# Fillers on an idle TensorE: from full products to short groups of transposes

## The chip, the core and the metric

The kernel runs on one core of a Trainium2 chip. The metric is the device time of one execution in microseconds (us). Before the change it is 1080.59 us, the median of 2 runs (1079.84 and 1081.34).

## The reference

A recurrent attention (RWKV-7) over 4 batches, 8 heads, 768 steps and a head size of 40 is followed by a gated feed-forward layer with 320 inputs and 1536 hidden units, all of it in fp32:

```python
for t in range(S):
    kt, vt, rt = (k[:, :, t], v[:, :, t], r[:, :, t])
    wt, at, bt = (w[:, :, t], a[:, :, t], b[:, :, t])
    y[:, :, t] = np.einsum('bhd,bhde->bhe', rt, state)
    Sa = np.einsum('bhde,bhe->bhd', state, at)
    state_decay = state * wt[:, :, None, :] - np.einsum('bhd,bhe->bhde', Sa, bt)
    state = state_decay + np.einsum('bhd,bhe->bhde', vt, kt)
...
rms = np.sqrt(np.mean(x * x, axis=-1, keepdims=True) + 1e-06)
xn = x / rms * rms_g
g = xn @ w_gate
silu = g * (1.0 / (1.0 + np.exp(-g)))
return (silu * (xn @ w_val) @ w_out)
```

Each batch and head has a state of 40 x 40 numbers; x is y with the heads of a time step side by side, 3072 rows of 320. The feed-forward weights come as 64-bit numbers, which the kernel narrows to fp32 itself.

## The kernel before

The 768 steps are cut into 24 chunks of 32. For each chunk there are four stages. `front` loads the chunk, turns it by transposes, and builds by levels (1, 2, 4, 8, 16 steps) the products between steps of the chunk: at each level TensorE multiplies `Ab` with `K` (a product on 40 rows and 64 columns), VectorE and ScalarE take the result into `LT` and `KN`, and make the `K` and `Ab` of the next level from those of this one. `inverse`, in the first chunks `early_inverse`, inverts a small triangular matrix of each sequence on VectorE. `main` takes the state through the chunk, forms y, normalizes it and transposes it into `xg`. After every second chunk `feed` multiplies 256 rows with the gate, value and output weights; that is most of TensorE's work. `narrow` makes the fp32 weights while the first chunks run.

Nothing is issued while these functions run. Each call of `tt`, `copy`, `pe` and so on adds a piece to a `Plan`. `Plan.issue` then walks through the text `ORDER`, which was written out ahead: each word is the place of the next piece among those left. It fixes the order on each engine, and there is no scheduler behind it. A word `-` stands for a filler: `self.warm()` is called, and one product goes to TensorE between two useful pieces. There are 151 such words in 33 runs of 1 to 14, all in the first quarter of the text. `PAIRS` says which of three pairs of PSUM banks each piece uses.

The filler is line 1017: the product of the identity with itself, 128 rows by 128 columns, accumulated into columns 320 to 447 of the first bank of `po`. `feed` uses columns 0 to 319 of both banks of `po` for its output; nothing ever reads the filler's columns. They are set to zero once, on line 519. An engine works through its queue in order, so a useful product behind fillers starts when they have gone through and its inputs are there.

Useful products are issued by line 488 (`mm`) and transposes by line 491 (`flip`); in fp32 a product is two instructions on TensorE and a transpose is one. Each has its own load of weights (LDWEIGHTS). Lines 446, 466, 469 and 472 are the helpers of VectorE and ScalarE.

Of the kernel before, what the change touches and what calls it, by code (L numbers as in the profile page):

```python
# [17 lines left out]
P = 128  # L18
# [352 lines left out]
def kernel(  # L371
# [33 lines left out]
    nc = tc.nc  # L405
    B, H, S, D = r.shape
    assert B == 4 and H == 8 and S % (CG * C) == 0 and D == 40
    DM = H * D
# [25 lines left out]
    def side(t, l, x):  # L434
# [4 lines left out]
    plan = Plan([psum.tile([P, 2, 512], FP32, name=f"ps{i}") for i in range(3)],  # L439
                [dram.tile([P, 2, 512], FP32, name=f"room{i}") for i in range(8)])  # L440
# [59 lines left out]
    ident = const.tile([P, P], FP32, name="ident")  # L500
# [15 lines left out]
    po_ = psum.tile([P, 2, 512], FP32, name="po")  # L516
    for t in plan.pairs[:2]:
        nc.vector.memset(t, 0.0)
    nc.vector.memset(po_[:, 0, DM:DM + P], 0.0)
    nc.scalar.copy(plan.pairs[2], plan.pairs[0])  # L520

    gcol = const.tile([P, KT], FP32, name="gcol")
# [107 lines left out]
    TOP = 64 + D  # L630
# [383 lines left out]
            front(c + 2)  # L1014
            (early_inverse if c + 2 < EARLY else inverse)(c + 2)

    plan.warm = lambda: nc.tensor.matmul(po_[:, 0, DM:DM + P], ident, ident, start=False, stop=False, skip_group_check=True)
    with tc.manual_schedule():
        plan.issue(ORDER, PAIRS)

# [29 lines left out]
```

## Time and profile before

| | before |
|---|---|
| median of the runs | 1080.59 us |
| the profiled execution: span from its first to its last instruction | 1078.2 us |
| TensorE busy (products) | 1010.2 us, 94% |
| TensorE busy (weight loads) | 828.3 us, 77% |
| VectorE, ScalarE, GpSimd busy | 834.2, 462.2, 309.0 us |
| mean granted clock of TensorE | 0.980 |
| fillers: product instructions | 302, first at 3.3 us, last at 233.9 us |
| duration of one such instruction (least, median, most) | 273, 275, 582 ns |
| fillers, busy | 47.3 us |

The profile holds one execution. Busy time counts each instruction with its latency, so instructions that follow each other closely overlap: the time from start to start is shorter than the duration. A row of the timeline merges instructions of one kind that follow each other, with the start of the first, the time to the end of the last, and their number; a bracket tells how long the engine stood idle before and what ended it. PEclk is the share of TensorE's full clock that was granted; the view in stretches gives its mean over each stretch. Ahead of the clock's first record, at 8.32 us, that view shows 1.00, though the instructions there have the durations of half the clock.

### The profile page before, as it was taken

What the parts mean: (1) busy time and instruction counts of PE and PEld (TensorE: products, weight loads), DVE (VectorE), ACT (ScalarE), POOL (GpSimd) and SP (SyncE); (2) the same over time, 40 slices, a digit from 0 to 9 for tenths busy, and PEclk for the clock granted to TensorE, in tenths of its full rate; (3) what the DMA queues carried; (4) which work ended last, traced back from release to release, by engine and by line L of the source; (5) the groups of instructions that cost most, each with busy time, mean ns of one, the idle gap of its engine ahead of it and who ended that gap; (6) DMA issues with size and microseconds to landing.
All of it is one profiled execution on the core that took longest, in us unless ns stands there. A gap on an engine that the chain in (4) does not pass through costs nothing. (4 is left out here: it accounts for less than half of the span.)

```text
span 1078.2 us, 53465 instructions
## 1 busy us (share of the span) xinstructions
PE 1010.2 (94%) x23406; PEld 828.3 (77%) x23406; DVE 834.2 (77%) x2861; ACT 462.2 (43%) x1043; POOL 309.0 (29%) x554
## 2 busy tenths in 40 slices
PE   6767899999999999999999999998999999999998
PEld 6766778777888787877788778887777887887776
DVE  7887879876868888887897888887788889797420
ACT  6845756643543433532443434433344344342211
POOL 9714404120532223241331331331332331200000
PEclk9778999999999999999999999999999999999999
DMA  9965448766564364574465654665545553744242
GB/s 180 196 155 123 73 106 220 213 127 177 124 142 122 99 150 116 144 145 120 96 152 133 146 126 112 142 142 123 126 106 110 134 150 90 162 109 123 77 140 86
DMA packets 172456, 143.34 MB, mean 133 GB/s; under 512 B 125504, under 2 KB 143872, under 8 KB 172224
## 3 DMA queue, kind: packets, MB, share of 16 engines
q1 hardware_dynamic: 153856, 116.96, 42.4%
q0 software_dynamic: 16192, 22.64, 12.2%
q8 instruction: 184, 3.01, 1.2%
q10 hardware_dynamic: 2176, 0.33, 0.2%
q14 instruction: 48, 0.39, 0.1%
HBM read 123.86 MB, written 15.99 MB: 130 GB/s over the span
## 5 line engine op out<-in xcount | busy, mean ns | idle before, releaser
L488 PE MATMUL ps<-xg,wf 128*128 128x256 f32 (+1 forms) x1728 | 355.2, 392 | 4.7 <-DVE xg L446 1.1
L488 PEld LDWEIGHTS ps<-xg,wf 128*128 128x128 f32 (+1 forms) x1728 | 261.6, 189 | 60.4 <-issue 16.9
L488 PE MATMUL po<-wf,hT 128*128 128x320 f32 x576 | 180.1, 445 | 0.1
L446 DVE TENSOR_TENSOR tmp<-Yi,M 128x60 f32<-128x60 f32 (+24 forms) x620 | 129.5, 209 | 19.7 <-DMA M<-sB 6.9
L446 DVE TENSOR_TENSOR Yi<-Yi,tmp 128x60 f32<-128x60 f32 (+24 forms) x620 | 130.2, 210 | 12.7 <-DVE ss L446 0.2
L466 ACT ACTIVATE sg<-ps 128x256 f32<-128x256 f32 x144 | 52.4, 383 | 192.4 <-PE ps L488 182.7
L488 PEld LDWEIGHTS po<-wf,hT 128*128 128x128 f32 x576 | 102.6, 191 | 34.0 <-issue 1.7
L485 POOL DMA_DIRECT2D VU<-in_v_dram x92 | 53.6, 587 | 234.2 <-PE ps L488 157.0
L446 DVE TENSOR_TENSOR hT<-ps,sg 128x256 f32<-128x256 f32 x144 | 59.0, 419 | 62.4 <-ACT sg L466 55.9
L469 ACT COPY KN<-ps 128x640 f32<-128x640 f32 x96 | 66.2, 691 | 76.6 <-PE ps L491 27.9
L488 PEld LDWEIGHTS ps<-Ab,K 40*64 40x64 f32 x4608 | 78.3, 139 | 26.4 <-issue 8.5
L446 DVE TENSOR_TENSOR K<-K,T 128x512 f32<-128x512 f32 (+1 forms) x192 | 93.3, 495 | 4.2 <-ACT K L469 2.1
L488 PE MATMUL ps<-Ab,K 40*64 40x56 f32 x4608 | 88.0, 225 | 8.8 <-ACT K L469 3.7
L485 POOL DMA_DIRECT2D kbn<-in_b_dram x92 | 53.4, 584 | 147.9 <-PE ps L488 147.0
L446 DVE TENSOR_TENSOR As<-ps,msi 128x256 f32<-128x256 f32 (+1 forms) x186 | 79.2, 475 | 18.3 <-PE ps L488 17.4
L469 ACT COPY K<-K 128x256 f32<-128x256 f32 (+1 forms) x168 | 71.8, 443 | 41.3 <-PE ps L488 20.3
L488 PEld LDWEIGHTS ps<-As,KN 128*40 128x40 f32 x3072 | 64.6, 122 | 15.1 <-issue 9.7
L485 POOL DMA_DIRECT2D wn<-in_w_dram x92 | 51.6, 565 | 83.7 <-DVE KN L446 34.7
L485 POOL DMA_DIRECT2D kbn<-in_k_dram x92 | 53.5, 585 | 73.8 <-PE ps L488 73.5
L488 PE MATMUL ps<-As,KN 128*40 128x32 f32 x3072 | 71.1, 203 | 3.7 <-issue 2.7
L446 DVE TENSOR_TENSOR y<-y,ps 128x256 f32<-128x256 f32 x119 | 49.9, 419 | 19.7 <-PE ps L488 17.6
L446 DVE COPY_PREDICATED LT<-near,ps 128x384 f32<-128x384 uint32 (+2 forms) x72 | 52.3, 727 | 3.6 <-PE ps L488 1.9
(133 smaller groups left out, 1544.5 us busy)
## 6 DMA issues: line engine op xcount, KB each, us to landing
wf<-sW SPq DMA_DIRECT2D x144, 480.0 KB, 4.3
M<-sB SPq DMA_DIRECT2D x80, 128.0 KB, 3.8
rn<-in_r_dram SPq DMA_DIRECT2D x24, 160.0 KB, 4.5
sW<-ex SPq DMA_DIRECT2D x16, 240.0 KB, 4.3
out_dram<-o SPq DMA_DIRECT2D x48, 80.0 KB, 3.9
kbn<-in_k_dram POOLq DMA_DIRECT2D x92, 40.0 KB, 3.5
kbn<-in_b_dram POOLq DMA_DIRECT2D x92, 40.0 KB, 3.3
wan<-in_a_dram POOLq DMA_DIRECT2D x46, 80.0 KB, 4.7
```

What stands on the lines that cost most here:

```text
L446: plan.add("DVE", kind, lambda at: fn(at(o), *m(at)), [o], aps(*args))
L466: plan.add("ACT", "act", lambda at: nc.scalar.activation(at(o), at(a), f, **kw), [o] + aps(acc), [a])
L469: plan.add("ACT", "copy", lambda at: nc.scalar.copy(at(o), at(a)), [o], [a])
L485: plan.add(by, "dma", lambda at: queue.dma_start(out=o, in_=i), [o], [i])
L488: return o, lhsT, rhs, lambda at: nc.tensor.matmul(at(o), lhsT, rhs, start=start, stop=stop, skip_group_check=True)
```

## The change

Each filler becomes a group of transposes of the identity, marked as transposes (`is_transpose`). Five kinds take turns, four fillers of each kind before the next. `D` is 40, `TOP` 104 and `P` 128.

| kind | rows | result rows | instructions of one filler |
|---|---|---|---|
| 1 | 64 | 128 | four of 64 columns, on the lower and upper 64 rows by turns |
| 2 | 40 | 128 | four of 40 columns, by turns as well |
| 3 | 64 | 104 | four of 64 columns, by turns as well |
| 4 | 64 | 104 | four of 64 columns, all on the lower 64 rows |
| 5 | 128 | 104 | one of 128 columns |

Those on the upper rows write to the second bank of `po`, so the memset of line 519 covers both banks. The words `-` stay where they are, and all other pieces and their order are unchanged on each engine.

```diff
-    nc.vector.memset(po_[:, 0, DM:DM + P], 0.0)
+    nc.vector.memset(po_[:, :, DM:DM + P], 0.0)
...
-    plan.warm = lambda: nc.tensor.matmul(po_[:, 0, DM:DM + P], ident, ident, start=False, stop=False, skip_group_check=True)
+    turns = [(64, P, 0), (D, P, 0), (64, TOP, 0), (64, TOP, 1), (P, TOP, 0)]
+
+    def warm():
+        kind = plan.fillers // 4 % len(turns)
+        plan.fillers += 1
+        rows_, cols, alone = turns[kind]
+        for _ in range(2 if rows_ < P else 1):
+            for i in range(1 if rows_ == P else 2):
+                u = 0 if alone else i
+                at = slice(u * 64, u * 64 + rows_)
+                nc.tensor.matmul(po_[0:cols, u, DM:DM + rows_], ident[at, 0:cols], ident[at, at], start=False, stop=False,
+                                 is_transpose=True, skip_group_check=True)
+
+    plan.fillers = 0
+    plan.warm = warm
```

## The prediction

> **What bounds the kernel now.** I read the page first (share of each engine, the span in 40 slices), then the groups of line 1017, which issues the fillers, then busy time in stretches of 3.41 us, then the timeline of TensorE around the runs of fillers. The page's chain of waits reaches back only to 785 us and consists mostly of TensorE's own products; it says nothing of the first 235 us, where all fillers lie, so that part is read from the stretches.
>
> From the page, a slice being 27 us:
>
> ```profile
> PE   6767899999999999999999999998999999999998
> DVE  7887879876868888887897888887788889797420
> PEclk9778999999999999999999999999999999999999
> ```
>
> TensorE is bound from the sixth slice on. In the first four it is not: it waits there for VectorE and ScalarE, and its granted clock is at 0.7 to 0.8. The same run in stretches of 3.41 us (busy time of each engine with its count, then the clock):
>
> ```profile
> core 0: us, PE busy (x) PEld busy (x) DVE busy (x) ACT busy (x) POOL busy (x), PEclk, DMA share, GB/s
> 25.39:28.80 3.41, 1.78 (x16) 1.79 (x17) 3.27 (x7) 3.34 (x8) 3.22 (x7) 1.00 1.20 242
> 32.22:35.63 3.41, 2.13 (x101) 1.64 (x101) 3.41 (x9) 3.41 (x10) 3.16 (x12) 1.00 1.04 240
> 35.63:39.04 3.41, 3.41 (x82) 3.08 (x78) 3.16 (x7) 3.35 (x8) 3.06 (x8) 0.50 0.69 154
> 49.28:52.70 3.42, 1.68 (x15) 1.49 (x14) 0.77 (x5) 3.36 (x8) 0.00 (x0) 1.00 1.10 278
> 73.18:76.59 3.41, 0.78 (x64) 0.69 (x64) 2.93 (x15) 0.26 (x1) 0.00 (x0) 1.00 0.60 136
> 76.59:80.00 3.41, 2.88 (x98) 2.46 (x99) 0.19 (x2) 0.80 (x3) 0.00 (x0) 0.50 0.89 280
> 83.42:86.83 3.41, 3.18 (x72) 2.67 (x72) 2.49 (x5) 3.32 (x5) 0.42 (x1) 0.50 0.16 15
> 86.83:90.24 3.41, 2.90 (x144) 2.56 (x145) 2.53 (x10) 3.38 (x7) 2.10 (x5) 1.00 0.53 131
> ```
>
> The clock changes only at these edges, between full and half. What decides is the streaming time, not busy time with its latency: a product instruction of n columns streams for 0.84 ns times n at full clock (128 columns: 107 ns, below), twice that at half. I counted it, overlaps once, for all stretches of the trace. Those after which the clock fell streamed 13, 31, 32, 32, 43 and 43% of the stretch; the lowest after which it stayed were 42, 44, 46, 47, 48%. At half clock it rose again after stretches with 82% or more and stayed down after 79% and less, and once after 86%. So the border is the same number of columns: 43% at full, some 85% at half clock. The stretches at 25.39, 49.28 and 69.76 stand at 47, 42 and 44%, of which fillers are 41, 42 and 44.
>
> What a product costs is read from the timeline (start, length of the merged row, tile, rows*columns of the weights, count):
>
> ```profile
> 28.57 1.04 PE L491 MATMUL ps<-ident,kbn 128*104 128x128 f32 x8
> 40.19 1.95 PE L491 MATMUL ps<-ident,wan 128*104 128x128 f32 x8
> 54.40 0.71 ACT L469 COPY K<-K 128x256 f32<-128x256 f32 x2 [0.24 <-DVE K L446]
> 53.91 2.27 PE L1017 MATMUL po<-ident 128*128 128x128 f32 x18
> 56.12 1.15 PE L488 MATMUL ps<-Ab,K 40*64 40x56 f32 x64
> 115.51 1.14 PE L488 MATMUL ps<-rE,vut 40*64 40x32 f32 x64 [0.21 <-ACT vut L469]
> 136.81 1.14 PE L488 MATMUL ps<-xg,wf 64*128 64x256 f32 x8
> 140.64 3.72 PE L488 MATMUL ps<-xg,wf 128*128 128x256 f32 x16
> ```
>
> A full transpose is one instruction: (1.04 - 0.27) / 7 = 0.11 us, at half clock (1.95 - 0.45) / 7 = 0.21. A filler is two instructions of 0.12 us: (2.27 - 0.28) / 17. Products on 64 rows run two side by side: (1.14 - 0.40) / 7 = 0.106 us against (3.72 - 0.39) / 15 = 0.222 on 128 rows.
>
> **The change part by part.** *Removed*: 151 fillers of two instructions at 0.115 us, some 34.7 us of TensorE. *Added*: 520 transposes for the same 151 places. The kind changes after every four fillers, so the five kinds come 32, 32, 31, 28 and 28 times. A transpose of 64 columns streams 0.055 us. Its weights of 128 columns must be loaded too: loads last 130 ns for 104 columns and 141 for 128, so 0.46 ns a column, 0.059 us for 128. That loads can be the limit is seen at 115.51: four side by side, (1.14 - 0.22) / 63 * 4 = 58 ns each, where 32 columns stream 27 ns. So a 64- or 40-row transpose takes about 0.06 us, and two halves side by side make a group of four 0.12 us. The fourth kind stays on one half, 0.24; the fifth is one full transpose, 0.11. Sum: 95 * 0.12 + 28 * 0.24 + 28 * 0.11 = 21.2 us. Transposes on 64 rows do not occur in this trace; were they not side by side, it would be 95 * 0.24 + 9.8 = 32.6. I take 21.2, since the nearest row, the 64-row products, overlaps. Either way they have no consumer; what counts is what follows.
>
> *TensorE is free earlier* (gain). At 56.12 the product starts when the fillers end, 1.0 us after its last input, the ScalarE copies that end at 55.11. Compared in this way with their last release, useful steps behind fillers start late by 1.0 (56.12), 0.9 (101.96), 0.75 (28.57), 0.7 (78.78), 0.6 (9.12), 0.6 (118.17) and 0.6 us (188.87), and all others together 1.2: 6.4 us. Some five of them go. Behind the remaining runs the input is late anyway, and shorter fillers only lengthen the wait.
>
> *The clock* (loss). Stretches whose fillers carry the border fall below it, and the next one runs at half clock, where useful streaming takes twice as long. At the start (3.3 us) fillers end at 5.1 instead of 6.85, TensorE waits for the load of wan, and the clock rises one stretch later: useful streaming there is 1.0 us, so +1.0. At 25.39 the fillers go from 41 to some 32%: next stretch +2.3. At 49.28 from 42 to 22%: +1.0. At 69.76 from 44 to 20-33%: +0.5. About even are 15.15 (60 to 43%, +2.2 at stake), 83.42 (82%, just at the upper border, so any shift of the starts decides; +2.1) and 192.64 (70 to 43%, +1.7); less likely 172.16 (61 to 45%, +1.7). With halves and a quarter: 4.8 + 3.0 + 0.4 = 8.2 us.
>
> *Code*. The page's instruction queue moved 184 packets for 46,812 TensorE instructions, one for some 256. In the first 250 us its weight loads wait for "issue" 37 times, 20.0 us, 0.54 each. 436 more instructions are 1.7 packets: +0.9 us at most, nothing if it falls into a wait; I take 0.5.
>
> *Memset*. One VectorE instruction of twice the columns ahead of the first filler; the first useful step waits for its load until 6.8 us in any case. Nothing. No wait, DMA or step on another engine is added or moved.
>
> *How much reaches the end.* In the front stage the next level's K is made by VectorE and ScalarE without TensorE; a product there only feeds LT and KN. With VectorE at 3.2 to 3.4 of 3.41 us in most of these stretches, some delay of TensorE is hidden, as is some gain. Between none and all I take half for both: -2.5 + 4.1 + 0.5 = +2 us. The profiled execution has a span of 1078.2, the median of the runs is 1080.59, 2.4 above, which I take as what lies around the span. Forecast **1082.5 us**, own range 1077 to 1092.
>
> **A rule that speaks against.** In the stretch at 83.42, eight full transposes and 64 products stream 82%, plain products alone 32%, and the clock rises behind it; at 76.59 plain products of 63% do not lift it. So transposes count here. The Trainium skill (TensorE: Matmul & The Clock Gate, section "Part 4: PE-mode transpose") says that transpose mode does not count as busy in the same way and does not bring the full clock. By that rule, not by this trace, the change would cost what the second rival below gives.
>
> **The rivals.**
> *Faster*: the clock holds, because half-array transposes count for more than I think or the edges fall kindly; then 5 us are gained, 1075.5. For it: the late starts. Against: three stretches stand within 4 points of the border and lose 9 to 22.
> *Transposes do not hold the clock*. Then it stays at half from the first filler until the dense products at 141 us. Useful streaming in stretches that are now at full clock before that is 10.3 + 2.9 + 0.5 + 6.4 + 20.9 = 41 us; it doubles: 1080.6 + 41 - 5 = 1116. It is slower by over 2% once 22 of the 41 us reach the end. Against: the stretch at 83.42, and 127.79, where plain products stream only 14% and the clock stays. The skill's rule is this rival.
> *It does little*: halves are not side by side, fillers are as long as before (32.6 against 34.7 us), and the stretches keep their share; with the code, 1081.
>
> **How the numbers follow.** Forecast 57%, little effect 18%, faster 15%, transposes not counted 7%, others 3%. About 2%, 21.6 us, is what a measurement of this kernel can tell from no change. Only the second rival lies beyond it, and not all of it: slower 0.07, faster 0.01, within 0.92. The range: all late starts gone and no clock lost, 1074.5; all clock losses on the path, each for two stretches, with the code, 1080.6 + 16.4 + 1 = 1098.
>
> **What would show it.** Right: a filler group of the first three kinds at 0.11 to 0.13 us between starts at full clock; half clock one stretch longer at the start and again behind the stretches near 25, 49 and 70 us; useful steps behind fillers starting at their release; after 240 us the same work in the same time. Wrong: groups of 0.24 us (loads or halves one after the other); full clock kept where the share falls under 40%; half clock where transposes stream over 50%; a chain that now waits for TensorE in the front stage, which would make the loss twice mine.

## The result, and the profile after

| | before | after |
|---|---|---|
| median of the runs | 1080.59 us | 1124.01 us (1119.0 and 1129.01) |
| ratio | | 1.040, 95% interval 1.029 to 1.051 |
| span of the profiled execution | 1078.2 us | 1126.7 us |
| mean granted clock | 0.980 | 0.944 |

The change costs 4.0%, some 43 us, where +2 us was forecast, with a range up to 1092 and an outer bound of 1098. Times of experiments below are ratios to the kernel before, run on the same chip; they leave out executions that the chip disturbed, so they need not equal a quotient of medians.

From the page of the changed kernel:

```profile
PE   5867898889999999999898999999989999999998
PEclk7757879999999999999999999999899999999999
q8 instruction: 186, 3.05, 1.2%
```

The clock is below nine tenths in the first six slices, of 28 us each, and again in the one at 789 us, where no filler has run for some 540 us. Lining up the useful products of both traces one by one (there are 23104 in each, in the same order) shows where the 48 us between the spans arise: the changed kernel is 0.9 us late at 102 us (in the times of the kernel before), where the sparse part ends; 5.8 at 132; 12.2 at 160; 18.2 at 257; and 48.5 at the last product. **Thirty of the 48 us arise behind the last filler**, in code that is the same.

There the waits differ. TensorE waiting for "issue", which is nothing that the profile shows (total, times, longest), from the view of waits of the whole execution, before (with the page's row of the queue):

```profile
q8 instruction: 184, 3.01, 1.2%
PE ps L488 <- issue: 21.9, 29, 1.9
```

and after:

```profile
PE ps L488 <- issue: 52.4, 41, 3.6
```

One such wait in the timeline of the changed kernel (start, length of the merged row, tile, rows*columns, count; idle time before it in brackets), and what follows:

```profile
160.19 1.09 PE L488 MATMUL ps<-rE,vut 40*64 40x32 f32 x64
161.21 0.93 PE L491 MATMUL ps<-ident,K 104*128 104x104 f32 x8
...
162.44 0.20 PE L488 MATMUL ps<-r,Sd 40*40 40x32 f32 x1
164.84 0.21 PE L488 MATMUL ps<-r,Sd 40*40 40x32 f32 x1 [2.19 <-issue]
...
165.51 0.46 PE L1027 MATMUL po<-ident 64*104 64x64 f32 x4
165.76 5.27 PE L488 MATMUL ps<-xg,wf 64*128 64x256 f32 x16
```

The same 16 products before the change:

```profile
154.75 0.70 PE L488 MATMUL ps<-xg,wf 64*128 64x256 f32 x4
156.17 2.63 PE L488 MATMUL ps<-xg,wf 64*128 64x256 f32 x12 [0.72 <-DMA sB<-LT]
```

In the middle of a step that waits for nothing, between two products of the same kind, TensorE stands still for 2.19 us. Then the 16 products take 5.27 us instead of 0.70 and 2.63. The stretches of 3.41 us (busy time of each engine, then the clock) tell why:

```profile
160.08:163.50 3.42, 2.56 (x128) 2.28 (x121) 2.92 (x7) 3.36 (x7) 0.00 (x0) 1.00 0.80 187
163.50:166.92 3.42, 2.08 (x38) 1.84 (x39) 1.30 (x4) 0.49 (x2) 0.21 (x1) 0.51 0.61 169
```

The standstill took streaming from the first stretch, and the clock's records show the next two at half clock. So a wait can be paid twice. Behind 260 us the clock of the changed kernel fell nine times before the end of the work. Of the stretches just before these falls, seven hold 1.6 to 2.8 us of waits like this one, and two hold none.

Where do these waits lie? Numbering TensorE's instructions in the order of the trace, weight loads and semaphore instructions included, **every** gap of over 0.6 us that is not a wait for a semaphore lies at a number 193 + 256k: 26 of 26 before, 38 of 38 after. The instruction queue moves packets of 16,384 bytes, one for 256 instructions, so these are the edges of code blocks. The packets themselves stand in the trace, and they settle what TensorE waits for: each of these 26 and 38 gaps ended 1.2 to 1.8 us, in the median 1.4, after the end of a packet of this queue. The standstill above ended at 164.84, behind a packet that ran from 162.37 to 163.25. Counting gaps over 0.15 us at edges, the sum is 36.9 us at 46 edges before and 69.2 us at 55 after. A block mostly comes late when TensorE runs through the one before too fast: of the blocks run through in under 2.5 us, 3 of 4 before and 12 of 16 after ended in a gap of over 0.6 us, of those that took 5 us and more 3 of 81 and 0 of 84. The change adds 436 instructions by 252 us, so every later edge falls 436 - 256 = 180 instructions earlier in the same code. More blocks then lie in sequences of small products (64 products with 64 loads in 1 us): 16 instead of 4 are run through in under 2.5 us.

### The profile page after: what moved, and what is told of

It is laid out like the page before. It is cut to its first block, busy times and chain, and to the rows that moved or that the text cites. A ratio compares the mean times of both kernels' runs of the same rounds, so it can differ in the third digit from the quotient of the medians.

```text
span 1126.7 us, 53901 instructions
## 1 busy us (share of the span) xinstructions
PE 1028.3 (91%) x23624; PEld 837.1 (74%) x23624; DVE 836.1 (74%) x2861; ACT 462.9 (41%) x1043; POOL 309.0 (27%) x554
## 5 line engine op out<-in xcount | busy, mean ns | idle before, releaser
L488 PE MATMUL ps<-xg,wf 128*128 128x256 f32 (+1 forms) x1728 | 362.0, 399 | 7.5 <-issue 2.8
L488 PEld LDWEIGHTS ps<-xg,wf 128*128 128x128 f32 (+1 forms) x1728 | 266.2, 193 | 65.3 <-issue 20.0
L488 PE MATMUL po<-wf,hT 128*128 128x320 f32 x576 | 184.7, 453 | 1.0 <-issue 0.9
L466 ACT ACTIVATE sg<-ps 128x256 f32<-128x256 f32 x144 | 52.4, 384 | 209.6 <-PE ps L488 203.9
L488 PEld LDWEIGHTS po<-wf,hT 128*128 128x128 f32 x576 | 104.9, 195 | 35.4 <-issue 3.9
L488 PEld LDWEIGHTS ps<-Ab,K 40*64 40x64 f32 x4608 | 81.1, 143 | 32.0 <-issue 18.9
L488 PE MATMUL ps<-Ab,K 40*64 40x56 f32 x4608 | 91.4, 230 | 14.1 <-issue 8.3
L469 ACT COPY KN<-ps 128x640 f32<-128x640 f32 x96 | 66.2, 690 | 83.5 <-PE ps L488 27.6
```

Source lines behind the costliest of these rows:

```text
L466: plan.add("ACT", "act", lambda at: nc.scalar.activation(at(o), at(a), f, **kw), [o] + aps(acc), [a])
L469: plan.add("ACT", "copy", lambda at: nc.scalar.copy(at(o), at(a)), [o], [a])
L488: return o, lhsT, rhs, lambda at: nc.tensor.matmul(at(o), lhsT, rhs, start=start, stop=stop, skip_group_check=True)
```

## The experiments

Two theories. *Code*: the edges of the blocks have moved. *Clock*: the shorter fillers, or their being transposes, hold the granted clock less. All kernels compute the full result. The sums at edges and the time at half clock behind each result are counted in its own trace, as above (before: 36.9 us and 45 us; after: 69.2 and 129; the clock's records end 2 to 3 us behind the span). A trace is one execution, and executions of one kernel differ by up to 2%, so small differences are read from the ratios alone.

**The shift alone, on whole fillers.** Small products that nobody reads are put behind the 78th filler, where TensorE waits 4.0 us for a DMA:

```diff
+    def pad(n):
+        for j in range(n):
+            at = slice(j % 4 * 32, j % 4 * 32 + 16)
+            nc.tensor.matmul(po_[at, 0, DM:DM + 16], ident[at, at], ident[at, at], start=False, stop=False, skip_group_check=True)
...
+        plan.fillers += 1
+        if plan.fillers == 78:
+            pad(45)
```

> The kernel before with its fillers untouched, and 45 products of 16x16 (90 products and 90 weight loads, 180 instructions, 0.9 to 3 us on an idle TensorE) behind the last filler of the run that ends at 71 us. Nothing else changes. Theory code: TensorE's instructions come in blocks of 256, and it stands still at block edges that it reaches too soon (36.9 us in all before, 69.2 us after); the change adds 436 instructions, so from 252 us on every edge lies 180 instructions further along the same code. Then this kernel has the edges of the changed kernel from 75 us on, and takes 1110 to 1130 us, with 60 to 70 us at block edges. Theory clock: the shorter fillers cost the time through the granted clock; then this kernel, whose fillers are whole, takes 1080 to 1084 us.

Measured: 1.032 (1.026 to 1.039). 60.6 us at edges, 41.5 of them behind 260 us (before 20.4, after 39.3). The waits, and the added products in the timeline:

```profile
PE ps L488 <- issue: 45.7, 42, 3.0
69.50 0.90 PE L1021 MATMUL po<-ident 16*16 16x16 f32 x90
```

The products take 0.9 us in a wait. Fillers as they were, edges as in the changed kernel: four fifths of the loss. (The forecast says "further along", and that for 224 instructions below "earlier"; both directions are reversed, since instructions that are added let an edge fall earlier in the code behind them. Its times do not depend on that.)

**The same with a whole block**, `pad(64)`:

> The kernel before with 64 products of 16x16 (256 instructions, one whole block) behind the last filler of the run that ends at 71 us. Theory code: every block edge behind it lies at the same instruction as before, so the time is that of before, 1079 to 1086 us, with 30 to 40 us at block edges. Rival: the products themselves, or more code as such, cost the 34 us of the kernel with 180 instructions; then this one, with more of them, takes 1115 to 1130 us.

Measured: 1.007 (1.004 to 1.011), 27.6 us at edges. Most of the loss is gone, though more was added. The page, and the waits:

```profile
PE   6868999999999999999999999999999999999998
PEclk9887999999999999999999999999999999999999
...
q8 instruction: 185, 3.03, 1.2%
```

```profile
PE ps L488 <- issue: 13.2, 22, 1.5
```

One more packet of code moves, and the waits are no more than before the change. This trace is of an execution of 1067.0 us, where the others took 1076.9 to 1088.9, so its low count says nothing of the remaining 0.7%, which stays open.

**Half a block**, `pad(32)`:

> The kernel before with 32 products of 16x16 (128 instructions, half a block) at the same place. Theory code: the edges lie half a block further along; they were at places that cost 36 us and 180 instructions further at places that cost 60 to 69 us, so this must lie well over 1081, at 1090 to 1130 us. If the time depends only on the count of instructions it lies between 0 and 180, near 1105 us.

Measured: 1.049 (1.046 to 1.052), 65.5 us at edges, 102 us at half clock, half of it behind 260 us. Fewer instructions than with 180, and slower:

```profile
PEclk9769998999999999999998999999989999999999
```

```profile
PE ps L488 <- issue: 52.3, 44, 3.3
```

The waits equal those of the changed kernel (52.4), with 128 instructions more than before instead of 436. What counts is the place, not the number.

**Near the old place**, `pad(8)` and `pad(56)`:

> The kernel before with 8 products of 16x16 (32 instructions) behind the last filler of the run that ends at 71 us. Theory code, with its cause: a block that TensorE runs through in less than some 4 us makes it wait for the next one. Adding up what each block of the trace of before lacks to 4 us, for edges moved along the code, gives 28 us where they lie now, 50 at 32 instructions, 70 at 96 (the most), 65 at 128 and 44 at 224. So 1095 to 1110 us here. If a move this small is harmless: 1080 to 1085.

Measured: 1.032 (1.026 to 1.039), 57.2 us at edges, 103 us at half clock; more than expected (1095 to 1110 us would be 1.1 to 2.5% over 1083, the median of before in that comparison).

> The same with 56 products (224 instructions, edges 32 instructions earlier than before, counted round). By the count of code added the time would lie at or above that of 180 instructions, 1115 us or more; by the edges it comes back towards before: 1088 to 1105 us.

Measured: 1.001 (0.996 to 1.005), 42.9 us at edges; by the ratio less than expected, or at the lower end of it (1088 to 1105 us would be 0.4 to 2.0% over 1083). The cost turns back before the block is full. Adding up what blocks lack to 4 us had given 22 us more at edges for 32 instructions and 16 more for 224; they became 20 and 6 more. With 32 instructions the time rose by some 35 us, more than the edges account for, and half clock by 58 us, which that sum leaves out; whether this is the whole difference is not shown. No place tried is faster than the old one.

**The changed kernel with its edges put back** from 252 us on, by 76 instructions more, `pad(19)` behind its 78th filler:

> The changed kernel with 19 products of 16x16 (76 instructions) behind the last filler of the run that ends at 74 us, so that 512 instructions, two whole blocks, are added in all. Theory code: from 252 us on the block edges lie where they lay before, and the 30 us that are lost behind 260 us come back; 1085 to 1100 us. Theory clock: only the fillers count, they are unchanged; 1119 to 1129 us as measured for the changed kernel.

Measured: 1.015 (1.008 to 1.022). The sum at edges is 38.8 us, 17.6 behind 260 us. The fillers are those of the change, the half clock in the first 104 us too (68 us of it, after 56), and most of the loss is gone:

```profile
PE ps L488 <- issue: 26.3, 24, 4.1
```

**With two paddings**, `pad(7)` behind the 78th and `pad(12)` behind the last filler:

> The changed kernel with 7 products of 16x16 behind the last filler of the run that ends at 74 us and 12 behind the very last filler. By then the change has added 228 and 464 instructions, so the edges stand at 256 and 512: between 75 and 100 us and from 252 us on they lie as before, between 100 and 252 us they wander by up to 208. Theory code: 1085 to 1100 us, nearer to 1085 if the rest of 15 us in the kernel with 76 instructions came from edges between 75 and 252 us. If that rest came from the clock it stays at 1096.

Measured: 1.011 (1.007 to 1.014); 18.1 us at edges behind 260 us, but 16.0 between 104 and 260 us, where the edges still wander (before: 5.3). Its interval overlaps that of the kernel with 76, so where the rest of 1.1 to 1.5% comes from, edges between 104 and 252 us or the clock, these two do not settle.

**Transposes or products, nothing moved.** Each filler as two full transposes:

```diff
-    plan.warm = lambda: nc.tensor.matmul(po_[:, 0, DM:DM + P], ident, ident, start=False, stop=False, skip_group_check=True)
+    def warm():
+        for _ in range(2):
+            nc.tensor.matmul(po_[:, 0, DM:DM + P], ident, ident, start=False, stop=False, is_transpose=True, skip_group_check=True)
```

> The kernel before with each filler made of two full transposes of 128 columns instead of one product: four instructions and 0.22 us as before, so that no block edge moves and the streaming time is the same. If transposes hold the clock as products do: 1079 to 1083 us. If transposes do not count for the clock (the rule that the prediction weighed): half clock until 141 us and 1105 to 1116 us. Theory code says 1080 to 1082.

Measured: 1.001 (0.997 to 1.005), with the clock of the early slices as high as before:

```profile
PEclk9688999999999999999999999999969999999999
```

The 6 far to the right is half clock of 17 us from 791 us on, 550 us behind the last filler. These transposes, in fp32, hold the clock as products do. The Trainium skill (TensorE: Matmul & The Clock Gate, section "Part 4: PE-mode transpose") says that transposes do not count as busy in that way; here the measurement decides against it.

**Shorter fillers, nothing moved.** Products of 64 columns instead of 128:

```diff
-... nc.tensor.matmul(po_[:, 0, DM:DM + P], ident, ident, ...
+... nc.tensor.matmul(po_[:, 0, DM:DM + 64], ident, ident[:, 0:64], ...
```

> The kernel before with the fillers' products cut from 128 to 64 columns: four instructions as before, so that no block edge moves, and half the streaming time. Theory code: all of the loss comes from the edges, so this takes what the prediction's clock and start terms give, 1076 to 1092 us, and the stretches near 25, 49 and 70 us are followed by half clock. Theory clock: the loss of the change is the fillers' shortness; 1110 to 1130 us.

Measured: 1.002 (0.999 to 1.006), 69 us at half clock, 52 of them before 104 us:

```profile
PEclk9766899999999999999999999999999999999999
```

One pair of half-array transposes for each filler, the change's first kind at half its length (with the memset of both banks):

```diff
+    def warm():
+        for u in range(2):
+            at = slice(u * 64, u * 64 + 64)
+            nc.tensor.matmul(po_[:, u, DM:DM + 64], ident[at, :], ident[at, at], start=False, stop=False,
+                             is_transpose=True, skip_group_check=True)
```

> The kernel before with each filler made of one pair of transposes of 64 rows and 64 columns side by side, 0.06 us instead of 0.23: four instructions as before, so that no block edge moves. It is the first kind of the change at half its length. Theory code: only the clock and the start terms are left, and the fillers hold the clock even less than in the change; 1081 to 1094 us, with 70 to 110 us at half clock. Theory clock: 1115 us or more.

Measured: 1.008 (1.005 to 1.011), 100 us at half clock.

```profile
PEclk8756699999999999999999999999999999999999
```

And fillers cut to one product of 16x16, `plan.warm = lambda: pad(1)`:

> The kernel before with each filler cut to a product of 16x16, four instructions as before: the fillers hold nothing, and no block edge moves. It prices the clock by itself. If half of the 41 us of useful streaming that the prediction counted reaches the end: 1095 to 1105 us. If what the halved products showed (24 us more at half clock, 2 us lost) goes on: 1083 to 1092 us.

Measured: 1.011 (1.004 to 1.017), 123 us at half clock. So all that the fillers' clock is worth is about 1%, a quarter of what the change lost. The short pairs had nearly the early clock of the changed kernel (65 us at half clock in the first 104, after 56), and cost 0.8%.

## Why the prediction was wrong

**The step that failed is "Code".** It took the 20.0 us of "issue" waits as a price per packet, 0.54 us, and put 1.7 packets more at "+0.9 us at most". The packets did become two more (184 to 186). But the waits are no price per packet. Of the 37 waits, 11 lie at block edges, with 11.8 of the 20.0 us; the others lie elsewhere in the code. And those at edges depend on where an edge lies in the code, and the change moves every edge behind its fillers. That term measured 1.032 by itself (the kernel with 180 instructions), about 35 us. With it falls the sign "after 240 us the same work in the same time".

**The fillers' length was right.** Groups at full clock take what was worked out:

```profile
10.71 1.21 PE L1027 MATMUL po<-ident 64*104 64x64 f32 x20
31.15 1.45 PE L1027 MATMUL po<-ident 40*128 40x40 f32 x32
```

The first row has one group of the third kind and four of the fourth: (1.21 - 0.26) / 19 * 4 = 0.20 us a group, worked out (0.12 + 4 * 0.24) / 5 = 0.22. The second has one of the second, four of the third and three of the fourth: 0.155 against 0.165. From start to start at full clock, groups of the first three kinds mostly took 0.11 to 0.13 us, those of the fourth 0.22. Half-array transposes do run side by side.

**The gate was right, with its border a little higher.** In the first 260 us of the changed kernel the clock fell after stretches that streamed 5, 29, 31, 44, 46 and 46%, and once, at 160.08, after 53%; the lowest after which it stayed were 47, 49 and 53%. It rose after stretches of 82% and more, once after 78%, and stayed at half after some of 81 to 87%, so the border is no sharp one. The stretch at 13.3 shows a fall of the predicted kind: its six fillers take 1.04 us, 1.60 before the change, it streamed 44%, and only 0.2 us of it are a wait at an edge:

```profile
13.31:16.72 3.41, 1.98 (x75) 1.67 (x75) 3.41 (x11) 0.95 (x3) 3.41 (x7) 1.00 1.25 163
16.72:20.14 3.42, 0.11 (x7) 0.00 (x0) 0.24 (x1) 0.58 (x1) 3.02 (x7) 0.51 1.12 201
```

The fall behind 57.7 has the other cause. There TensorE stands at an edge for 3.62 us from 59.3 on, in the middle of a run of fillers, and 2.2 of them are in this stretch:

```profile
57.69:61.10 3.41, 1.59 (x67) 1.22 (x66) 3.34 (x11) 1.72 (x3) 0.00 (x0) 1.00 1.01 179
61.10:64.52 3.42, 1.61 (x22) 1.27 (x22) 3.35 (x12) 3.39 (x8) 1.32 (x3) 0.51 0.09 14
```

Behind the three places that the prediction named, near 25, 49 and 70 us, no fall is seen in this execution: their code comes later here, and the clock was at half already, up to 30.5 and 54.4 us at the first two and all along at the third. At the start the clock rose at 9.9 instead of 8.3 us, not a full stretch later: the grid of stretches lay 1.6 us later in that execution, and the stretch from 6.6 us was filled to 84%.

**The share that reaches the end was about right for the sparse part.** Half clock in the first 104 us went from 34 to 56 us, 27 of them behind that stretch at 57.7, and the useful products were only 0.9 us late there. Halved products, at 52 us of half clock, cost 0.2%, within the forecast of +2 us; fillers that hold nothing cost 1.1%. "Half" is not excluded by any of these.

**The rivals.** "Transposes do not hold the clock", at 1116 us the nearest to the measured time, is refuted by the two full transposes: a near time with a wrong cause. "Little effect" and "faster" fall. No rival had the cause. It was in reach: the gaps at 193 + 256k were in the trace of before, and part of their total had been quoted.

## What to carry to other kernels

Instructions that cost nothing where they stand can cost several per cent elsewhere, because they move the edges of code blocks through everything behind them. Before judging a change that adds or removes instructions on a dense engine, put its number back to a whole block, 256 here, with instructions in a wait; else one measures the shift with the change. An order that was tuned by time may be tuned for its edges too, which no run here shows. An engine that runs through sequences of very small instructions is the one to look at.

## What was not expected of the hardware

- TensorE stood still at the edges of 256-instruction blocks for up to 3.9 us (changed kernel), and its other gaps of over 0.6 us were all waits for semaphores. In each of the thirteen traces every edge gap of over 0.6 us ended 1.1 to 1.8 us after the end of a 16,384-byte packet of the instruction queue. 32 more instructions in a wait of the kernel before cost 3.2%, 256 cost 0.7%.
- Such waits of some 2 us in a stretch of 3.41 us often lower the granted clock for the next one (seven of nine falls behind 260 us). Behind 260 us the changed kernel had 34 us at half clock instead of 7, with no filler near: 18.9 us more at edges and half of the 27 us more at half clock make 32.5, of the 30 us that arose there.
- Transposes in fp32 count for the clock as products do (1.001 with all fillers exchanged), and fillers at all are worth about 1.1% here.
- Left open: what sets the start of a packet (0.7 to 4.9 us behind the edge before, where a gap of over 0.6 us followed, before and after the change), and the 0.7% of the kernel with a whole block more.
